# A banded attention with a feed-forward block on one core: operands of TensorE moved by a few words inside SBUF

## The chip, the cores and the metric

The kernel runs on one core of one Trainium2 chip. The metric is the device time of one execution in microseconds (us). "Word" below means 4 bytes, "place" means the start address of an operand in a partition of SBUF modulo 256 bytes, given in words (0 to 63).

## The reference

```python
scores = scale * (q @ k.T)                     # B=4, H=8, S=768, D=64
keep = (pos_k < n_sink) | (0 <= pos_q - pos_k < window)   # 4 sinks, window 128
a = softmax(where(keep, scores, -1e9)); x = a @ v          # x: 3072 tokens x 512
h = x @ w_in                                   # 512 -> 2048
out = (h - tanh(h)) @ w_out                    # 2048 -> 512
```

All operands are float32.

## The kernel before, in words

The 3072 tokens are cut into 12 chunks of 256. A chunk's attention makes its activations x, transposed (4 blocks of 128 features by 256 tokens). They are split into a rounded high part and a low part, `xh` and `xl`, and both lie in one half of the tile `xall` (chunk 2 alone has tiles of its own). A chunk then goes through 8 steps, one for each group of 256 hidden features. 96 steps `n` follow one another; `order` lists them: first chunks 0 to 2, taken in turn, then chunks 3 to 11, each with its 8 groups.

The first product of a step (`mm1`, L807) is 24 matmuls of 128x128 by 256 columns: a block of `w_in` is loaded as weights, and a block of `xh` or `xl` is streamed past it. Chunks 0 to 2 read `w_in` from tiles that stay in SBUF (`w0_g`). The later chunks get it by DMA into a ring of 7 slots, four in the tile `ring`, three in `spare`. ScalarE and VectorE then make the gate h - tanh(h) and split it again (`gate`): into `ghbuf` (high) and `glbuf` (low).

The second product has two forms. In steps of chunks 0 to 4, and in the last step (`mm2`, L877, 12 matmuls of 512 columns), halves of `ghbuf` and `glbuf` are the weights, and `w_out` is streamed. Steps with even `n` use the first half of `glbuf`, steps with odd `n` the second (`halves`). In the other steps (`mm7`, L911, 21 matmuls of 256 columns in a Strassen scheme) seven blocks of `ghbuf` and `glbuf` are the weights; blocks of `w_out` or of the tiles `edge` are streamed.

All instructions are recorded in a list with the engine, an estimated duration, a due time and the resources that they read and write. `Work.order` plays this list once and fixes the order of each engine; the waits between engines are then set by which bytes of a tile an instruction reads or writes. While one matmul streams, TensorE already loads the weights of the next one.

Places before, from the layout that the program is built with. `xall` begins at place 0. Chunks 0 and 1 lie 16 words into their half of it, so at place 16, and the chunks from 3 on at 0. The weights `w0_g` are at 0, but the tile that holds `w0_1` and later `ring` is at 16, as are `spare`, `ghbuf` and `glbuf`. `w_out` and the `edge` tiles are at 0. The key operands `ks` of the scores (L524) start at 0, 4, 32 or 36, their queries `q` at 16.

Of the kernel before, what the change touches and what calls it, by code (L numbers as in the profile page):

```python
# [9 lines left out]
F32 = mybir.dt.float32  # L10
F32R = mybir.dt.float32r
# [7 lines left out]
P = 128  # L19
# [20 lines left out]
@with_exitstack  # L40
def kernel(
    ctx: ExitStack,
    tc: tile.TileContext,
    qd: bass.AP,
    kp: bass.AP,
    vp: bass.AP,
    vs: bass.AP,
    nsw: bass.AP,
    w_in: bass.AP,
    w_out: bass.AP,  # L50
    xd: bass.AP,
    out: bass.AP,
):
    nc = tc.nc

    cpool = ctx.enter_context(tc.tile_pool(name="cpool", bufs=1))
    ident = cpool.tile([P, P], F32, tag="ident", name="ident")
    nswi = cpool.tile([P, 32], I32, tag="nswi", name="nswi")[:, :4]

    pts = cpool.tile([P, NPAIR, 2, 4, P], F32, tag="pt", name="pt")  # L60
    early = []
    for m in range(2):
        first = pts[:, m].rearrange("p h a b -> p (h a b)")
        early.append((first[:, :KW], first[:, KW : KW + 2 * CH].rearrange("p (h s) -> p h s", h=2)))
    et = mybir.EngineType
    with tc.manual_schedule(engines={et.PE, et.SP, et.DVE, et.Activation, et.Pool}):

        scr = pts[:, 2, 0]
        nc.sync.dma_start(nswi, nsw.partition_broadcast(P))
        for m in range(2):  # L70
            k, q = early[m]
            nc.sync.dma_start(k, kp[0, m, :, :KW])
            _load_pair(nc, q, qd[0, 2 * m : 2 * m + 2, :, :CH], True)
            if m == 0:
                make_identity(nc, ident)
                nc.gpsimd.iota(scr[:, 0, :].bitcast(I32), pattern=[[-1, P]], base=0, channel_multiplier=1)
                nc.gpsimd.iota(scr[:, 1, :].bitcast(I32), pattern=[[1, P]], base=0, channel_multiplier=0)
        masks = _masks(nc, cpool, nswi, scr)
        _, (nlo, nhi, wlo, whi) = nc.values_load_multi_w_load_instructions(
            nsw[0:1, 0:4], skip_runtime_bounds_check_because="every value takes one of the two branches"  # L80
        )
        bad = nhi | whi | ((nlo + 3) >> 3) | ((wlo - 1) >> 7)


        WARM = 3
        with tc.tile_pool(name="warm", bufs=1, space=PSUM) as wp:
            warm = wp.tile([P, P], F32, tag="warm", name="warm")
            for _ in range(WARM):
                nc.tensor.matmul(warm, lhsT=ident, rhs=ident, start=True, stop=True)

    with tc.If(bad == 0) as cmp:
        _banded(tc, qd, kp, vp, vs, masks, w_in, w_out, ident, pts, early, out)
    with cmp.Else():
        _general(tc, qd, kp, vp, nswi, w_in, w_out, ident, xd, out)

# [8 lines left out]
        nc.sync.dma_start(q[r, h, :], src[h, r])  # L104


def _masks(nc, pool, nswi, scr):

    mask = pool.tile([P, 3, TS], F32, tag="mask", name="mask")
    above = pool.tile([P, P], F32, tag="above", name="above")
    below = pool.tile([P, P], F32, tag="below", name="below")
    after = pool.tile([P, P], F32, tag="after", name="after")
    lim = pool.tile([P, 2], F32, tag="lim", name="lim")
    diff, col, tmp = (scr[:, i, :] for i in range(3))
    nc.gpsimd.memset(mask[:, 0, :NSK], NEG)
    nc.vector.tensor_copy(diff, diff.bitcast(I32))
    nc.vector.tensor_copy(col, col.bitcast(I32))  # L120
    nc.vector.tensor_scalar(above, diff, 0.0, None, op0=ALU.is_lt)
    nc.vector.tensor_scalar(below, diff, 0.0, None, op0=ALU.is_le)
    nc.vector.tensor_scalar(after, diff, 0.0, None, op0=ALU.is_gt)
    nc.vector.scalar_tensor_tensor(diff, above, float(P), diff, op0=ALU.mult, op1=ALU.add)
    nc.vector.tensor_scalar(tmp, above, NEG, None, op0=ALU.mult)
    nc.vector.tensor_copy(lim[:, 0:1], nswi[:, 0:1])
    nc.vector.tensor_copy(lim[:, 1:2], nswi[:, 2:3])
    n_sink, window = lim[:, 0:1], lim[:, 1:2]
    nc.vector.tensor_scalar(mask[:, 2, NSK:], diff, window, NEG, op0=ALU.is_ge, op1=ALU.mult)
    nc.vector.tensor_scalar(col, col, n_sink, NEG, op0=ALU.is_ge, op1=ALU.mult)  # L130
    nc.vector.tensor_tensor(mask[:, 0, NSK:], mask[:, 2, NSK:], tmp, op=ALU.min)
    nc.vector.tensor_tensor(mask[:, 0, NSK:], mask[:, 0, NSK:], col, op=ALU.max)

    near, edge, sink = diff[:, :NSK], tmp[:, :NSK], col[:, :NSK]
    nc.vector.tensor_scalar(near, near, window, None, op0=ALU.is_lt)
    nc.vector.tensor_tensor(edge, edge, near, op=ALU.mult)
    nc.vector.tensor_tensor(mask[:, 1, :NSK], edge, sink, op=ALU.min)

    def rest():
        nc.scalar.copy(mask[:, 1, NSK:], mask[:, 2, NSK:])  # L140
        nc.scalar.copy(mask[:, 2, :NSK], sink)

    return mask, above, below, after, rest
# [86 lines left out]
        return sorted(start, key=lambda n: (start[n], n)), start  # L230


def _banded(tc, qd, kp, vp, vs, masks, w_in, w_out, ident, pts, early, out):
    nc = tc.nc
    et = mybir.EngineType
    with ExitStack() as ctx:
# [6 lines left out]
        bpool, wmpool, qpool, kpool, hpool, xpool = (  # L243
            pool(n, 1) for n in ("bpool", "wmpool", "qpool", "kpool", "hpool", "xpool")
        )
        pp, sm = pool("pp", 2), pool("sm", 4)
        xall = xpool.tile([P, 4 * NPAIR * CH + 16], F32R, tag="xall", name="xall")
        ps, ps_h = pool("ps", 1, space=PSUM), pool("ps_h", 2, space=PSUM)
        dpool = pool("dpool", 1, space=bass.MemoryType.DRAM)

        banks = {n: ps.tile([P, 512], F32, tag=n, name=n) for n in ("s0", "s1", "o0", "o1", "t", "x")}
# [4 lines left out]
        flat = wide.rearrange("p a b c -> p (a b c)")  # L256
        gbuf = gpool.tile([P, 8, P], F32, tag="gbuf", name="gbuf")
        ghbuf = gpool.tile([P, 2, 7, P], F32R, tag="ghbuf", name="ghbuf")
        glbuf = gpool.tile([P, 8, P], F32R, tag="glbuf", name="glbuf")
        wscr = dpool.tile([NG, P, 2 * WG], F32, tag="wscr", name="wscr")  # L260
        bscr = dpool.tile([NG, P, 5, DM // 2], F32, tag="bscr", name="bscr")
        kscr = dpool.tile([2, P, 2, DM // 2], F32, tag="kscr", name="kscr")
# [150 lines left out]

        sides = cpool.tile([P, 4], F32, tag="sides", name="sides")
        sidei = cpool.tile([P, 16], I32, tag="sidei", name="sidei")[:, :4]
        half, odd = sides[:, 0:2], sides[:, 2:4]
        vsink = cpool.tile([P, 2, P], F32R, tag="vsink", name="vsink")
        vraw = cpool.tile([P, P], F32, tag="vraw", name="vraw")  # L420
# [86 lines left out]
        def scores(u, t):  # L507
# [134 lines left out]
        def attend(cc, p0, pairs):  # L642
# [35 lines left out]
            def x_high(i):  # L678
                if p0 == 0 and i == 0:
# [1 line left out]
                        xh[cc] = bpool.tile([P, NPAIR, CH], F32R, tag="hb", name=f"xh{cc}")  # L681
                        xl[cc] = hpool.tile([P, NPAIR, CH], F32R, tag="ha", name=f"xl{cc}")
                    else:
                        at = 2 * NPAIR * CH * (1 - home(cc)) + 16 * (cc < 3)
                        both = xall[:, at : at + 2 * NPAIR * CH].rearrange("p (k n c) -> p k n c", k=2, n=NPAIR)
                        xh[cc], xl[cc] = both[:, 0], both[:, 1]
                r = slice(p0 + 2 * i, p0 + 2 * i + 2)
# [126 lines left out]

        def halves(n):
            r = n % 2
            return ghbuf[:, r].rearrange("p b t -> p (b t)")[:, : 2 * CH], glbuf.rearrange("p b t -> p (b t)")[:, r * 2 * CH : (r + 1) * 2 * CH]

        def gate(n):
            g0 = gbuf.rearrange("p b t -> p (b t)")[:, : 2 * CH]  # L820
# [542 lines left out]
```

## Time and profile before

| | |
|---|---|
| time, median of 3 runs | 678.68 us (678.13, 678.68, 681.78) |
| profiled execution: span from first to last instruction | 676.2 us |
| what the median has beside that span | 2.5 us |
| TensorE busy with matmuls | 655.5 us (97%) |
| VectorE, ScalarE, GpSimd busy | 531.8, 412.6, 204.0 us |

The profile states no time for the profiled execution but its span; the 2.5 us are taken as what lies around it. Matmuls are pipelined: a row of a matmul gives a duration of some 280 ns for 256 columns, while the next begins some 115 ns after it. The distance from start to start (the "beat") is therefore read from the timeline, as the time between the starts of two rows divided by the matmuls between them. The duration of a single matmul follows the beat and is used where only durations are grouped.

### The profile page before, as it was taken

Reading aid. Unit: us, or ns where it says so; the run is one execution under the profiler, and the core shown is the slowest. Engines: PE = TensorE matmul, PEld = TensorE weight load, DVE = VectorE, ACT = ScalarE, POOL = GpSimd, SP = SyncE. Lnnn points to the kernel's source line nnn. Section 1 sums busy time; section 2 is a strip of 40 time slices with the busy share of each in tenths; the row PEclk is TensorE's granted clock in tenths of the full one; section 3 lists DMA queues with packets and bytes.
Section 4 is the critical chain, followed back from the end, with each engine's and each line's share of the span. In section 5 each row is a group of like instructions: output and inputs, shape, how many; then the busy total and the mean of one; then the engine's idle time right before and its main releaser. Section 6 shows DMA issues by size and latency. Waiting matters only on the chain.

```text
span 676.2 us, 14570 instructions
## 1 busy us (share of the span) xinstructions
PE 655.5 (97%) x5099; PEld 603.3 (89%) x5099; DVE 531.8 (79%) x1365; ACT 412.6 (61%) x1056; POOL 204.0 (30%) x363
## 2 busy tenths in 40 slices
PE   6899999999999999999999999999999999999995
PEld 4677899998988899889999999999999999999995
DVE  6889998964898975567798898888988878855654
ACT  4986443435998876556776667567667567632331
POOL 5454000001995443344523323332223322300100
PEclk9999999999999999999999999999999999999998
DMA  5878797786998677799977767867777766657861
GB/s 177 266 262 269 266 295 263 270 287 175 191 203 274 203 217 223 227 280 266 300 217 240 224 199 207 260 196 203 227 231 216 242 199 199 198 165 207 270 198 37
DMA packets 79341, 152.96 MB, mean 226 GB/s; under 512 B 9564, under 2 KB 25564, under 8 KB 79260
## 3 DMA queue, kind: packets, MB, share of 16 engines
q1 hardware_dynamic: 65884, 121.65, 57.4%
q0 software_dynamic: 13376, 30.30, 16.4%
q8 instruction: 42, 0.69, 0.4%
q14 instruction: 39, 0.32, 0.1%
HBM read 131.47 MB, written 20.45 MB: 225 GB/s over the span
## 4 chain that ended last, share of the span: by engine, by line
PE 73%; ACT 7%; DVE 5%; DMA 5%; POOL 4%; issue 4%; POOLq 0%; SPq 0%; DVEq 0%; ACTq 0%
PE h L807 30%; PE s L911 10%; PE o L911 7%; PE o L877 6%; PE x L672 3%; PE s L877 3%; DMA w<-bscr 2%; PE t L609 2%; PE t L672 2%; PE t L877 2%; PE t L524 2%; PE x L877 2%; ACT p L575 2%; PE x L524 1%; ACT p L549 1%
## 5 line engine op out<-in xcount | busy, mean ns | idle before, releaser
L807 PE MATMUL h<-xall,ring 128*128 128x256 f32 x990 | 130.9, 279 | 0.0
L807 PEld LDWEIGHTS h<-xall,ring 128*128 128x128 f32 x990 | 121.2, 188 | 0.9 <-PE t L672 0.2
L826 ACT ACTIVATE gbuf<-h 128x512 f32<-128x512 f32 x96 | 57.1, 595 | 84.6 <-PE h L807 55.2
L356 POOL DMA_DIRECT2D qraw<-qd x36 | 29.3, 813 | 222.4 <-DVE q L496 198.0
L807 PE MATMUL h<-xall,spare 128*128 128x256 f32 x738 | 96.2, 277 | 0.0
L807 PEld LDWEIGHTS h<-xall,spare 128*128 128x128 f32 x738 | 90.0, 188 | 0.5
L549 ACT ACTIVATE p<-p,st 128x132 f32<-128x132 f32 x168 | 66.9, 400 | 26.8 <-DVE st L541 25.5
L845 ACT CAST ghbuf<-gbuf 128x896 fp32r<-128x896 f32 x55 | 51.9, 943 | 49.3 <-DVE gbuf L842 48.8
L848 DVE TENSOR_TENSOR glbuf<-gbuf,ghbuf 128x896 fp32r<-128x896 f32 x55 | 60.3, 1096 | 19.7 <-ACT ghbuf L845 16.0
L575 ACT ACTIVATE p<-p,st 128x132 f32<-128x132 f32 x168 | 54.2, 394 | 3.9 <-DVE st L570 3.5
L829 DVE TENSOR_TENSOR gbuf<-h,gbuf 128x512 f32<-128x512 f32 x55 | 37.8, 687 | 19.1 <-ACT gbuf L826 18.7
L877 PE MATMUL o<-w,ghbuf 128*128 128x512 f32 x192 | 50.8, 399 | 0.3
L629 POOL TENSOR_TENSOR pt<-pt,after 128x512 f32<-128x512 f32 x32 | 44.4, 1386 | 22.0 <-ACT pt L626 21.3
L807 PE MATMUL h<-xall,w 128*128 128x256 f32 x384 | 50.5, 282 | 0.0
L807 PEld LDWEIGHTS h<-xall,w 128*128 128x128 f32 x384 | 48.5, 188 | 1.6
L829 DVE TENSOR_TENSOR h<-h,gbuf 128x512 f32<-128x512 f32 x41 | 28.5, 694 | 19.1 <-ACT gbuf L826 19.0
L488 DVE TENSOR_TENSOR ks<-kraw,ks 64x392 fp32r<-64x392 f32 x72 | 40.4, 562 | 3.4 <-ACT ks L483 1.1
L877 PEld LDWEIGHTS o<-w,ghbuf 128*128 128x128 f32 x192 | 33.8, 188 | 6.8 <-ACT ghbuf L832 0.9
L623 DVE TENSOR_TENSOR pt<-t,below 128x512 f32<-128x512 f32 (+1 forms) x48 | 28.8, 600 | 12.6 <-PE t L609 7.4
L483 ACT CAST ks<-kraw 64x392 fp32r<-64x392 f32 x72 | 37.1, 515 | 2.2 <-DMA kraw<-kp 1.4
L911 PE MATMUL s<-edge,ghbuf 128*128 128x256 f32 x220 | 35.5, 280 | 0.1
L835 DVE TENSOR_TENSOR glbuf<-h,ghbuf 128x512 fp32r<-128x512 f32 x41 | 28.1, 685 | 9.1 <-ACT ghbuf L832 9.1
(174 smaller groups left out, 1560.8 us busy)
## 6 DMA issues: line engine op xcount, KB each, us to landing
ring<-wscr SPq DMA_DIRECT2D x165, 256.0 KB, 4.3
spare<-wscr SPq DMA_DIRECT2D x123, 256.0 KB, 4.6
qraw<-qd POOLq DMA_DIRECT2D x36, 256.0 KB, 5.0
wraw<-w_in SPq DMA_DIRECT2D x16, 512.0 KB, 6.0
wraw<-w_out SPq DMA_DIRECT2D x16, 512.0 KB, 5.7
wscr<-w SPq DMA_DIRECT2D x16, 512.0 KB, 6.0
kraw<-kp POOLq DMA_DIRECT2D x36, 196.0 KB, 4.6
v<-vp POOLq DMA_DIRECT2D x18, 256.0 KB, 3.4
```

The lines of the kernel that those rows point to most:

```text
L483: nc.scalar.copy(ks[u][r, h, :], kt[u][r, :])
L488: (nc.gpsimd if KP else nc.vector).tensor_tensor(k[o, h, :], t[r, :], k[r, h, :].bitcast(F32), op=ALU.subtract)
L549: nc.scalar.activation(e, e, AF.Exp, bias=st[u][:, j : j + 1], scale=-1.0, accum_out=st[u][:, 4 + j : 5 + j],)
L575: nc.scalar.activation(pr[u][:, j, :], pr[u][:, j, :], AF.Copy, scale=s[:, 8 + j : 9 + j])
L629: nc.gpsimd.tensor_tensor(w[:, :, 0, :], w[:, :, 0, :], after.unsqueeze(1).to_broadcast([P, 4, P]), op=ALU.mult)
L807: nc.tensor.matmul(hps[n][:, f, :], lhsT=w, rhs=x, start=r == 0, stop=r == 11)
L826: nc.scalar.activation(g0, h(), AF.Tanh)
L829: nc.vector.tensor_tensor(g0 if strassen(n) else h(), h(), g0, op=ALU.subtract)
L845: nc.scalar.copy(ghbuf[:, n % 2], gbuf[:, 1:, :])
L848: nc.vector.tensor_tensor(glbuf[:, :7, :], gbuf[:, 1:, :], ghbuf[:, n % 2].bitcast(F32), op=ALU.subtract)
L877: nc.tensor.matmul(sums_of(n, cc, t), lhsT=a[:, f, t * P : (t + 1) * P], rhs=wt[1, g][:, (0, 1, 0)[i], f, :], start=first and not low and ...
L911: nc.tensor.matmul(acc, lhsT=a[:, b, :], rhs=factor(g, m, part % 2), start=g == 0 and part == 0 and m in (4, 1, 2, 7), stop=closes(n) and ...
```

## The change

The change moves tiles and slices, and leaves every computation as it is.

- Activations: the chunk's slice in `xall` starts at `xoff(cc)` words: chunks 0 and 1 at 48 (16 before), the chunks 3 to 11 at 1, 36, 2, 46, 16, 43, 20, 42 and 24 (0 before). `xall` is 32 words longer. Slices of neighbouring chunks do not overlap.
- Halves of the gate (steps with `mm2` alone): both halves start `shift(n)` words later, with 32, 30, 28, 26 and 4 in turn, so at places 48, 46, 44, 42 and 20 (16 before). `glbuf` gets 32 more words and another pool. The blocks that `mm7` reads stay at 16.
- Room for that: four small tiles (`lim`, `sides`, `sidei`, one of the four `st`) become slices of the tile of `nswi`, and the other three `st` become one tile.

```diff
-    nswi = cpool.tile([P, 32], I32, tag="nswi", name="nswi")[:, :4]
+    small = cpool.tile([P, 32], I32, tag="nswi", name="nswi")
+    nswi = small[:, :4]
...
-    lim = pool.tile([P, 2], F32, tag="lim", name="lim")
+    nswi, lim = small[:, :4], small[:, 4:6].bitcast(F32)
...
-        xall = xpool.tile([P, 4 * NPAIR * CH + 16], F32R, tag="xall", name="xall")
+        SHIFT, XOFF = 32, 48
+        xall = xpool.tile([P, 4 * NPAIR * CH + XOFF], F32R, tag="xall", name="xall")
...
+        stats = sm.tile([P, 3, 12], F32, tag="st", name="st")
+        glflat = cpool.tile([P, SHIFT + 8 * P], F32R, tag="glbuf", name="glbuf")
+        glbuf = glflat[:, : 8 * P].rearrange("p (b t) -> p b t", b=8)
...
-        glbuf = gpool.tile([P, 8, P], F32R, tag="glbuf", name="glbuf")
...
+        def xoff(cc):
+            return (48, 48, 0, 1, 36, 2, 46, 16, 43, 20, 42, 24)[cc]
+
+        def shift(n):
+            return (32, 30, 28, 26, 4)[n % 5]
...
-                    st[u] = sm.tile([P, 12], F32, tag="st", name=f"st{u}")
+                    st[u] = stats[:, u % 4] if u % 4 < 3 else small[:, 20:32].bitcast(F32)
...
-                        at = 2 * NPAIR * CH * (1 - home(cc)) + 16 * (cc < 3)
+                        at = 2 * NPAIR * CH * (1 - home(cc)) + xoff(cc)
...
             r = n % 2
-            return ghbuf[:, r].rearrange("p b t -> p (b t)")[:, : 2 * CH], glbuf.rearrange("p b t -> p (b t)")[:, r * 2 * CH : (r + 1) * 2 * CH]
+            a, b = shift(n), shift(n) + r * 2 * CH
+            return ghbuf[:, r].rearrange("p b t -> p (b t)")[:, a : a + 2 * CH], glflat[:, b : b + 2 * CH]
```

The order of instructions on every engine is the same; what is new is 18 waits. The two halves of `glbuf` were apart before. Now, where the shift changes from one step to the next, the half that VectorE writes in a step can share 2 to 28 words with the half that TensorE reads for the step before. The rows that follow are VectorE's around the low part of the gate in step 7 (`glbuf<-h`), of the kernel before:

```order
L829 TENSOR_TENSOR h_1204<-h_1204,gbuf 128x512 [waits Activation_49]
L158 SCALAR_TENSOR_TENSOR pt<-wraw_4_975,pt 128x1024 [waits DVE_49]
L835 TENSOR_TENSOR glbuf<-h_1204,ghbuf 128x512 [waits Activation_49]
L160 SCALAR_TENSOR_TENSOR pt<-wraw_4_975,pt 128x1024 [waits DVE_49]
L156 TENSOR_SCALAR pt<-wraw_4_1030 128x1024 [waits DMAHW3_49,DMAHW7_49,DMAHW2_49,DMAHW0_49]
```

The same place of the changed kernel:

```order
L840 TENSOR_TENSOR h_1190<-h_1190,gbuf 128x512 [waits Activation_49]
L159 SCALAR_TENSOR_TENSOR pt<-wraw_4_961,pt 128x1024 [waits DVE_49]
L846 TENSOR_TENSOR glbuf<-h_1190,ghbuf 128x512 [waits PE_49,Activation_49]
L161 SCALAR_TENSOR_TENSOR pt<-wraw_4_961,pt 128x1024 [waits DVE_49]
L157 TENSOR_SCALAR pt<-wraw_4_1016 128x1024 [waits DMAHW3_49,DMAHW7_49,DMAHW2_49,DMAHW0_49]
```

Nothing moved, but the low part now waits for TensorE as well; 16 of the 41 low parts of `mm2` steps do. The decoding of weights (`pt<-wraw`) is queued behind it. In two other steps (17 and 33) the low part stands ahead of the matmuls that read the other half, and there the last of these matmuls waits for VectorE. On TensorE, at the end of the second product of step 16, the changed kernel has:

```order
L888 MATMUL x<-w_7_1597,ghbuf 128x512 x4
L888 MATMUL t<-w_7_1597,glbuf 128x512 [waits DVE_49]
L888 MATMUL t<-w_7_1597,glbuf 128x512
L888 MATMUL x<-w_7_1597,glbuf 128x512
L888 MATMUL x<-w_7_1597,glbuf 128x512 [waits DVE_49]
```

The last two rows were one row `x2` without a wait.

## Rows read from the trace of the kernel before

**Rows 1.** The page: span and TensorE's busy time, its granted clock.

```profile
span 676.2 us, 14570 instructions
...
PEclk9999999999999999999999999999999999999998
```

**Rows 2.** Windows: us of window, busy us of each engine (instructions), clock.

```profile
77.50:202.40 124.90, 123.79 (x822) 110.75 (x822) 101.37 (x188) 69.65 (x162) 34.14 (x49) 1.00 0.82 244
202.40:318.00 115.60, 115.05 (x812) 102.35 (x811) 83.66 (x241) 80.76 (x221) 50.05 (x84) 1.00 0.81 239
318.00:664.00 346.00, 344.79 (x3036) 334.56 (x3036) 275.88 (x701) 204.90 (x484) 87.74 (x151) 1.00 0.72 218
```

**Rows 3.** Groups of TensorE: count, busy us, mean ns of one, idle before.

```profile
L807 PE MATMUL h<-xall,ring 128*128 128x256 f32 x990 | 130.9, 279 | 0.0
L807 PE MATMUL h<-xall,spare 128*128 128x256 f32 x738 | 96.2, 277 | 0.0
```

**Rows 4.** TensorE's timeline, chunk 10: start, us, what, count.

```profile
609.60 0.84 PE L807 MATMUL h<-xall,spare 128*128 128x256 f32 x6
610.28 2.20 PE L807 MATMUL h<-xall,ring 128*128 128x256 f32 x18
612.32 0.62 PE L911 MATMUL s<-edge,ghbuf 128*128 128x256 f32 x4
...
614.70 0.84 PE L807 MATMUL h<-xall,ring 128*128 128x256 f32 x6
```

**Rows 5.** TensorE's timeline, chunk 5, step 42.

```profile
334.47 0.87 PE L807 MATMUL h<-xall,ring 128*128 128x256 f32 x6
335.17 1.58 PE L807 MATMUL h<-xall,spare 128*128 128x256 f32 x12
336.59 0.63 PE L911 MATMUL s<-edge,ghbuf 128*128 128x256 f32 x4
337.06 0.40 PE L911 MATMUL o<-edge,ghbuf 128*128 128x256 f32 x2
```

**Rows 6.** TensorE's timeline, chunk 1, step 13.

```profile
126.92 2.99 PE L807 MATMUL h<-xall,w 128*128 128x256 f32 x24
129.75 1.10 PE L877 MATMUL t<-w,ghbuf 128*128 128x512 f32 x4
```

**Rows 7.** Line 807 by operands: count, min/median/max ns; whole late stretch, then step 42.

```profile
L807 PE MATMUL h<-xall,ring x990: 276/276/388, 205.0 to 663.5; 128*128 128x256 f32 x198
L807 PE MATMUL h<-xall,spare x738: 276/276/374, 209.1 to 662.8; 128*128 128x256 f32 x185
...
L807 PE MATMUL h<-xall,spare x12: 281/281/281, 335.2 to 336.5; 128*128 128x256 f32 x12
```

**Rows 8.** Line 807 by operands, 77.5 to 212, then step 4 (75.9 to 81.3).

```profile
L807 PE MATMUL h<-xall,w x306: 276/279/365, 77.8 to 192.7; 128*128 128x256 f32 x153
L807 PE MATMUL h<-xh,w x112: 274/279/284, 81.8 to 148.9; 128*128 128x256 f32 x112
L807 PE MATMUL h<-xl,w x56: 279/283/290, 81.9 to 148.8; 128*128 128x256 f32 x56
...
L807 PE MATMUL h<-xall,w x24: 276/282/283, 76.1 to 81.2; 128*128 128x256 f32 x24
```

**Rows 9.** Line 524 by operands, 202 to 664.

```profile
L524 PE MATMUL t<-ks,q x96: 277/283/396, 279.6 to 580.7; 128*128 128x260 f32 x96
L524 PE MATMUL x<-ks,q x96: 278/283/385, 279.9 to 580.9; 128*128 128x260 f32 x96
```

**Rows 10.** Line 877 by operands, 60 to 318.

```profile
L877 PE MATMUL o<-w,ghbuf x177: 388/394/502, 59.8 to 315.9; 128*128 128x512 f32 x177
L877 PE MATMUL s<-w,ghbuf x64: 390/394/401, 64.6 to 160.5; 128*128 128x512 f32 x64
```

**Rows 11.** Timelines of VectorE and TensorE, step 7.

```profile
98.54 0.68 DVE L835 TENSOR_TENSOR glbuf<-h,ghbuf 128x512 fp32r<-128x512 f32 x1
...
98.25 0.63 PE L877 MATMUL x<-w,glbuf 128*128 128x512 f32 x2
...
103.43 1.09 PE L877 MATMUL s<-w,glbuf 128*128 128x512 f32 x4
```

**Rows 12.** Timelines of VectorE and TensorE, steps 17 and 16.

```profile
155.09 0.69 DVE L835 TENSOR_TENSOR glbuf<-h,ghbuf 128x512 fp32r<-128x512 f32 x1 [0.65 <-ACT ghbuf L832]
...
155.60 0.63 PE L877 MATMUL x<-w,glbuf 128*128 128x512 f32 x2
```

More of the change, by code (lines that the diff above doesn't have):

```diff
@@ L77 @@
                 nc.gpsimd.iota(scr[:, 1, :].bitcast(I32), pattern=[[1, P]], base=0, channel_multiplier=0)
-        masks = _masks(nc, cpool, nswi, scr)
+        masks = _masks(nc, cpool, small, scr)
         _, (nlo, nhi, wlo, whi) = nc.values_load_multi_w_load_instructions(
@@ L91 @@
     with tc.If(bad == 0) as cmp:
-        _banded(tc, qd, kp, vp, vs, masks, w_in, w_out, ident, pts, early, out)
+        _banded(tc, qd, kp, vp, vs, small, masks, w_in, w_out, ident, pts, early, out)
     with cmp.Else():
@@ L104, in _load_pair, with _masks @@
         nc.sync.dma_start(q[r, h, :], src[h, r])
-def _masks(nc, pool, nswi, scr):
+def _masks(nc, pool, small, scr):
     mask = pool.tile([P, 3, TS], F32, tag="mask", name="mask")
@@ L230, in order, with _banded @@
         return sorted(start, key=lambda n: (start[n], n)), start
-def _banded(tc, qd, kp, vp, vs, masks, w_in, w_out, ident, pts, early, out):
+def _banded(tc, qd, kp, vp, vs, small, masks, w_in, w_out, ident, pts, early, out):
     nc = tc.nc
@@ L245, in _banded @@
         )
-        pp, sm = pool("pp", 2), pool("sm", 4)
-        xall = xpool.tile([P, 4 * NPAIR * CH + 16], F32R, tag="xall", name="xall")
+        pp, sm = pool("pp", 2), pool("sm", 1)
+        SHIFT, XOFF = 32, 48
+        xall = xpool.tile([P, 4 * NPAIR * CH + XOFF], F32R, tag="xall", name="xall")
         ps, ps_h = pool("ps", 1, space=PSUM), pool("ps_h", 2, space=PSUM)
+        stats = sm.tile([P, 3, 12], F32, tag="st", name="st")
+        glflat = cpool.tile([P, SHIFT + 8 * P], F32R, tag="glbuf", name="glbuf")
+        glbuf = glflat[:, : 8 * P].rearrange("p (b t) -> p b t", b=8)
         dpool = pool("dpool", 1, space=bass.MemoryType.DRAM)
@@ L412, in _banded @@
             qt[u], kt[u] = q, k
-        sides = cpool.tile([P, 4], F32, tag="sides", name="sides")
-        sidei = cpool.tile([P, 16], I32, tag="sidei", name="sidei")[:, :4]
+        sides = small[:, 8:12].bitcast(F32)
+        sidei = small[:, 16:20]
         half, odd = sides[:, 0:2], sides[:, 2:4]
```

## The prediction, made before the changed kernel ran

> **What bounds the kernel now.** I read the page first: TensorE is busy for nearly the whole span, at the full granted clock (2.4 GHz) up to the last slice [rows 1]. The windows say where: from 77.5 to 202.4 us it is busy 123.79 of 124.90 us, from 202.4 to 318 us 115.05 of 115.60, from 318 to 664 us 344.79 of 346.00 [rows 2]. VectorE, the next, has 19% of the first stretch to spare and more of the others. So the time is the number of matmuls times the beat from one start to the next, and every ns on a beat is paid in full. The change has no other lever: it moves no instruction and only changes places, so the question is whether the beat depends on places.
>
> It does, or on something that goes with them. In chunk 10 two steps start 5.10 us apart (609.60 and 614.70) with 24 + 21 matmuls between, a beat of 113.3 ns [rows 4]. In step 13, which has the same matmul with other places (activations at 16 words, weights at 0), 24 matmuls take from 126.92 to 129.75, a beat of 117.9 ns [rows 6]. No engine is waited for in either. The durations follow: 276 ns on the fast beat, 279 to 282 on the slow one [rows 7, 8]. But places are not all. In step 42 the places are those of chunk 10, and 18 matmuls take from 334.47 to 336.59, 117.8 ns each, 281 ns long [rows 5, 7]. There is thus a fast and a slow beat, and at the places of the late chunks both can hold, the fast one nearly always: the median of all late matmuls is its 276 ns [rows 7].
>
> Of the places that the trace shows, only activations at 0 with weights at 16, 16 words behind the weights, are fast. At 16 with weights at 0 the median is 279; at 0 with weights at 0 (`xl` of chunk 2) 283; at 16 with weights at 16 (step 4) 282 [rows 8]. The score matmuls, with keys at 0, 4, 32 and 36 and queries at 16, have 283 [rows 9]; their 4 more columns are worth 4/256 of 113 ns, 2 ns, so these are slow as well, though they come in runs too short to settle.
>
> **The change part by part.** The sum is made on the span of 676.2 us; the median lies 2.5 us above it, and that is added at the end.
>
> *First products of the nine late chunks.* 990 + 738 = 1728 matmuls, 192 a chunk [rows 3]. What they take now: the means are 277 ns at `spare` and 279 at `ring`, where single ones behind a wait last up to 388 [rows 3, 7]. I take the 277, 1 ns above the fast duration, so a mean beat of 114.3. On the slow beat a chunk loses 117.8 - 114.3 = 3.5 ns x 192 = 0.67 us. None of the new places is shown by the trace except one: chunk 7, at 16 with weights at 16, is the case of step 4, which is slow. Measured by the distance to the weights, chunks 3 and 5 (at 1 and 2) move from -16 to -15 and -14, next to the fast place; chunks 7, 9 and 11 (16, 20, 24) go to 0, +4 and +8; chunk 4 (36) to +20; chunks 10, 8 and 6 (42, 43, 46) to +26, +27 and +30. At 0 and +16 the rows are slow, so I count 7, 9, 11 and 4 as slow. Of +26 to +30 nothing is known, and I count them with the nearest row, +16. Seven slow chunks: 7 x 0.67 = +4.7 us. Bounds: all nine slow, +6.0; all on the fast beat without a slip, 1728 x 1 ns = -1.7.
>
> *Second products behind them.* The 21 matmuls of a step in chunks 5 to 11 keep their places and could run fast, but step 42 shows that a slow beat is handed on: after its first product, 4 matmuls of L911 take from 336.59 to 337.06, 117.5 ns [rows 5]. Six of the seven slow chunks have this form: 6 x 8 steps x 21, about 1000 matmuls. If a quarter stays slow: 250 x 3.5 ns = +0.9 us. Bounds 0 and 3.5 us.
>
> *Chunks 0 and 1.* They move from 16 to 48 with weights at 0, so from a distance of +16 to +48, which is -16 modulo 64: the distance of the late chunks. 306 matmuls of this kind lie in the stretch where TensorE bounds [rows 2, 8], 24 of them (step 4) with weights at 16. The other 282 gain 117.9 - 113.3 = 4.6 ns, -1.3 us. Bounds: nothing; or, if they become as `xl` of chunk 2, 283 for 279 ns, +4 ns, +1.1 us. I take -1.3, as the distance is the only reading that I use above.
>
> *The halves of the gate.* 41 steps x 12 = 492 matmuls of 512 columns, whose weights move from 16 to 20 and 42 to 48. Their median is 394 ns in every stretch and whatever their neighbours are, between 388 and 401 apart from waits [rows 10]. A matmul twice as long covers the load of the next weights for longer, so I take 0. Bounds: all at the shortest, 492 x 6 = -3.0 us; all at the longest, 492 x 7 = +3.4 us.
>
> *The 18 new waits.* In step 7 the low part starts on VectorE at 98.54, and the matmuls that read the other half end at 98.25 + 0.63 = 98.88: a wait of 0.34 us. Behind it stands the decoding of weights, and its own reader starts only at 103.43, 4.2 us after the low part ends [rows 11]. VectorE has 23 us to spare in that stretch [rows 2], so this is hidden: 0. Without that cover, 16 waits of 0.34 us would be 5.4 us. Where TensorE waits, in step 16, the low part ends at 155.09 + 0.69 = 155.78, and the second of the two matmuls from 155.60 on would start at about 155.83 [rows 12]: 0, at most some 0.1 us. The merged small tiles change no instruction, 0.
>
> Sum: 4.7 + 0.9 - 1.3 = +4.3; 676.2 + 4.3 + 2.5 = 683.0 us.
>
> **A rule against this.** The late chunks and step 13 run the same matmul at 113.3 and 117.9 ns with nothing else waited for [rows 4, 6]. The Trainium skill, TensorE: Matmul & The Clock Gate, section "Step-by-step: what each phase is for", says that TensorE has two independent read ports into SBUF and that loading the next weights takes no bandwidth from the running matmul. By that rule places would be worth nothing, and the sum would be 0: that is the first rival, and the trace bears it out only in so far as both beats occur at the same places.
>
> **The rivals.**
>
> *Places do not decide.* The beat is set by how loads and matmuls fall against one another after a wait, and the places only happen to differ between the stages. For it: step 42 [rows 5]. Against it: step 13 and its like stay slow throughout, and the late chunks return to 276 after each disturbance [rows 7, 8]. The time is then 678.7, give or take 1.5 us.
>
> *Only a start at a multiple of 256 bytes is fast.* For it: every row with activations at 16 is slow, whatever the weights [rows 8]. Against it: `xl` of chunk 2 starts at 0 and is slow, with weights at 0. Then all nine chunks lose, +6.0 us; a quarter of all second products follows, 1155 x 1/4 x 3.5 = +1.0; chunks 0 and 1 gain nothing. 676.2 + 7.0 + 2.5 = 685.7 us, and 688.7 if all second products follow.
>
> *The new places are the better ones* (the other side). Most late chunks hold the fast beat without a slip (-1.7), the second products slip less with them (1155 x 1 ns, -1.2), chunks 0 and 1 gain 1.3, and the halves come near their shortest duration (up to -3.0). That is 674.5 without the halves and 671.5 with them. It decides from the point where no more than one of the nine is slow and the halves give 1 us or more. Against it: nothing in the trace is below 276 ns for long, so there is little to win, and each place that is shown, other than today's, is slow.
>
> **How the numbers follow.** The forecast (four to seven chunks slow) has 0.38, 680.5 to 685.5; the rule of 256 bytes 0.20, 685 to 689; no effect of places 0.24, 677 to 680.5; better places 0.18, 671 to 676. A change of under 0.5%, 3.4 us, cannot be told from none, so faster is below 675.3 and slower above 682.1. Faster: most of the last case, 0.15. Slower: two thirds of the first and nearly all of the second, 0.25 + 0.19 = 0.44. The rest, 0.41, is no change. The range that leaves out no more than 2 in 10 goes from 674 to 687.5.
>
> **What would show it.** Grouped by chunk, the first products should have a median of 276 ns in chunks 3 and 5 and of 281 in 4, 7, 9 and 11; chunks 6, 8 and 10 decide between 680.5 and the full sum. Step 13 should take 2.72 us for its 24 matmuls, not 2.83. The 512-column rows should stay at 394, and idle time of TensorE before `glbuf` should not grow. The prediction is wrong if the durations of the late chunks do not move, if they fall below 276, or if the 512-column matmuls change by more than 2 ns.

## The result, and the profile after

The changed kernel takes 685.59 us (median of 7 runs, 683.02 to 687.03), the kernel before in the same comparison 679.59 us. The ratio is 1.0083, 95% interval 1.0056 to 1.0110: slower by 0.8%. The profiled span grew from 676.2 [rows 1] to 683.8 us. In every run on record the time lies 1.7 to 1.9 us above the span, so the profiled execution of the kernel before took about 678.1 us, the lowest of its seven runs (678.13). Some 0.6 of the 2.5 us that the prediction adds are therefore that execution's distance from the median. It lies 1.5 us below the median of the seven, which is why the spans differ by 7.6 us and the medians by 6.0.

The windows of the changed kernel, cut at the same steps as before (columns as in rows 2):

```profile
76.80:201.30 124.50, 122.91 (x822) 109.99 (x820) 101.83 (x188) 69.52 (x161) 33.87 (x49) 1.00 0.81 245
201.30:318.00 116.70, 116.28 (x806) 103.83 (x807) 83.30 (x239) 81.24 (x222) 50.34 (x84) 1.00 0.81 236
318.00:671.50 353.50, 352.95 (x3041) 343.10 (x3040) 276.97 (x703) 204.56 (x484) 87.21 (x151) 1.00 0.70 214
```

Against [rows 2] the three stretches changed by -0.4, +1.1 and +7.5 us. The granted clock is 1.00 in all (2.4 GHz) as before and TensorE's busy time grew with the stretch, so the loss is in the late steps and in the beat. By operands, the page of after (columns as in rows 3):

```profile
L817 PE MATMUL h<-xall,ring 128*128 128x256 f32 x990 | 135.8, 284 | 0.0
...
L817 PE MATMUL h<-xall,spare 128*128 128x256 f32 x738 | 100.1, 283 | 0.0
...
L817 PE MATMUL h<-xall,w 128*128 128x256 f32 x384 | 49.8, 281 | 0.0
```

L817 is L807 of before. The late first products went from 279 and 277 ns [rows 3] to 284 and 283. Chunk by chunk (count, min/median/max ns, first and last start; chunks 3 to 11 in turn, `ring` alone):

```profile
L817 PE MATMUL h<-xall,ring x120: 278/283/362, 204.2 to 258.7; 128*128 128x256 f32 x120
...
L817 PE MATMUL h<-xall,ring x102: 277/281/362, 264.8 to 314.9; 128*128 128x256 f32 x102
...
L817 PE MATMUL h<-xall,ring x114: 279/283/365, 318.3 to 368.2; 128*128 128x256 f32 x114
...
L817 PE MATMUL h<-xall,ring x110: 278/285/366, 374.2 to 422.7; 128*128 128x256 f32 x110
...
L817 PE MATMUL h<-xall,ring x110: 274/283/364, 422.4 to 474.1; 128*128 128x256 f32 x110
...
L817 PE MATMUL h<-xall,ring x114: 276/282/384, 479.7 to 528.1; 128*128 128x256 f32 x114
...
L817 PE MATMUL h<-xall,ring x104: 275/280/365, 531.1 to 580.5; 128*128 128x256 f32 x104
...
L817 PE MATMUL h<-xall,ring x120: 278/284/364, 580.4 to 629.3; 128*128 128x256 f32 x120
...
L817 PE MATMUL h<-xall,ring x102: 277/280/357, 633.9 to 671.0; 128*128 128x256 f32 x102
```

No chunk kept the 276 of [rows 7]: none of the nine places holds the fast beat for a chunk. The beat itself, in chunk 10 (TensorE's timeline of after, answering to rows 4):

```profile
605.52 1.60 PE L817 MATMUL h<-xall,spare 128*128 128x256 f32 x12
606.96 1.60 PE L817 MATMUL h<-xall,ring 128*128 128x256 f32 x12
608.40 0.62 PE L922 MATMUL s<-edge,ghbuf 128*128 128x256 f32 x4
...
610.78 1.60 PE L817 MATMUL h<-xall,ring 128*128 128x256 f32 x12
```

The 24 first products take 2.88 us, 120.0 ns each, and the 21 second products behind them 2.38 us, 113.3 ns. In this chunk the loss sits on the matmuls whose operand was moved, and on no other.

The other direction, step 13, which answers to rows 6:

```profile
125.97 2.89 PE L817 MATMUL h<-xall,w 128*128 128x256 f32 x24
128.70 1.08 PE L888 MATMUL t<-w,ghbuf 128*128 128x512 f32 x4
```

2.73 us for 24 matmuls where it was 2.83, a beat of 113.8 ns. Step 19, at the same places, has 117.8 ns for 18 matmuls (160.42 to 162.54):

```profile
160.42 2.29 PE L817 MATMUL h<-xall,w 128*128 128x256 f32 x18
162.54 0.64 PE L534 MATMUL s<-ks,q 128*128 128x260 f32 x4
```

So at 48 past weights at 0 both beats occur. Of the 14 steps of chunks 0 and 1 past weights at 0, nine have 113.3 to 114.9 ns and five 117.4 to 117.9 (the first two distances of each left out); before, all 14 were at 117.5 to 117.9. VectorE's new waits (line waited for: us in total, times, longest):

```profile
DVE glbuf L846 <- PE o L888: 3.9, 3, 1.5
...
DVE glbuf L846 <- PE x L888: 1.0, 3, 0.4
```

Its wait for `ghbuf` at the same line fell from 9.1 to 7.1 us. TensorE waits for `glbuf` as long as before, 0.8 us once (before, then after):

```profile
PE t L877 <- DVE glbuf L835: 0.8, 1, 0.8
...
PE t L888 <- DVE glbuf L846: 0.8, 1, 0.8
```

From here on a beat is a mean over the distances from one start to the next, with the distances that hold a wait left out; I worked them out from the timelines. The beats explain the loss:

| matmuls | count | before | after | us |
|---|---|---|---|---|
| first products, chunks 3 to 11 | 1728 | 114.19 | 119.34 | +8.9 |
| second products behind them (L922) | 1155 | 114.11 | 115.25 | +1.3 |
| first products, chunks 0 and 1 | 384 | 117.88 | 115.79 | -0.8 |
| 512 columns, halves of the gate | 492 | 233.10 | 231.64 | -0.7 |

The sum is +8.7 us. The distances with a wait in them, which stand beside these, became about 1 us shorter in all, which leaves about the 7.6 us of the span. Two profiles of one kernel differ by about 1 us in the opening alone (before: the first product starts at 42.6 and at 41.5 us), so I read effects under 2 us from beats, not from spans.

### The profile page after: what moved, and what is told of

It reads as the page before. It is cut to its first block, busy times and chain, and to the rows that moved or that the text cites. A ratio compares the mean times of both kernels' runs of the same rounds, so it can differ in the third digit from the quotient of the medians.

```text
span 683.8 us, 14585 instructions
## 1 busy us (share of the span) xinstructions
PE 664.5 (97%) x5099; PEld 613.7 (90%) x5099; DVE 532.3 (78%) x1365; ACT 412.8 (60%) x1056; POOL 204.0 (30%) x363
## 4 chain that ended last, share of the span: by engine, by line
PE 80%; DVE 6%; ACT 4%; DMA 3%; POOL 3%; issue 2%; SPq 0%; POOLq 0%; DVEq 0%; ACTq 0%
PE h L817 35%; PE s L922 11%; PE o L922 8%; PE o L888 7%; PE x L682 3%; PE s L888 3%; PE t L619 2%; PE t L534 2%; PE t L682 2%; PE t L888 2%; PE x L534 2%; PE x L888 2%; DMA kraw<-kp 2%; DMA w<-bscr 1%; DVE pt L633 1%
## 5 line engine op out<-in xcount | busy, mean ns | idle before, releaser
L817 PE MATMUL h<-xall,ring 128*128 128x256 f32 x990 | 135.8, 284 | 0.0
L817 PEld LDWEIGHTS h<-xall,ring 128*128 128x128 f32 x990 | 125.3, 189 | 0.8 <-PE t L682 0.2
L817 PE MATMUL h<-xall,spare 128*128 128x256 f32 x738 | 100.1, 283 | 0.0
L817 PEld LDWEIGHTS h<-xall,spare 128*128 128x128 f32 x738 | 93.3, 190 | 0.5
L559 ACT ACTIVATE p<-p,st 128x132 f32<-128x132 f32 x132 | 52.6, 401 | 21.7 <-DVE st L551 20.6
L817 PE MATMUL h<-xall,w 128*128 128x256 f32 x384 | 49.8, 281 | 0.0
L817 PEld LDWEIGHTS h<-xall,w 128*128 128x128 f32 x384 | 47.8, 188 | 1.5
L585 ACT ACTIVATE p<-p,st 128x132 f32<-128x132 f32 x132 | 42.6, 394 | 3.2 <-DVE st L580 2.8
L922 PE MATMUL s<-edge,ghbuf 128*128 128x256 f32 x220 | 35.9, 282 | 0.0
```

Source lines behind the costliest of these rows:

```text
L559: nc.scalar.activation(e, e, AF.Exp, bias=st[u][:, j : j + 1], scale=-1.0, accum_out=st[u][:, 4 + j : 5 + j],)
L585: nc.scalar.activation(pr[u][:, j, :], pr[u][:, j, :], AF.Copy, scale=s[:, 8 + j : 9 + j])
L817: nc.tensor.matmul(hps[n][:, f, :], lhsT=w, rhs=x, start=r == 0, stop=r == 11)
L922: nc.tensor.matmul(acc, lhsT=a[:, b, :], rhs=factor(g, m, part % 2), start=g == 0 and part == 0 and m in (4, 1, 2, 7), stop=closes(n) and ...
```

## The experiments

All but e5_before_again and g1_high48 are the changed kernel with other numbers in `xoff` (first line of each diff: places of chunks 0 to 11) and `shift` (second line: 0 keeps the halves at 16, 32 puts them at 48, 28 at 44); e4_ring32 has a line more. What most gave stands in one table (beats in ns); "all" is the median time, with the 95% interval of the ratio to the kernel before where the two were timed side by side.

| kernel | all, us | 95% of the ratio | late first | second | chunks 0, 1 | 512 col. | chunk 10, 11 |
|---|---|---|---|---|---|---|---|
| before | 679.59 | | 114.19 | 114.11 | 117.88 | 233.10 | 113.7, 113.4 |
| after | 685.59 | 1.0056 to 1.0110 | 119.34 | 115.25 | 115.79 | 231.64 | 119.9, 116.8 |
| e1_late_only | 685.32 | 1.0057 to 1.0183 | 119.34 | 115.20 | 117.87 | 233.22 | 120.0, 116.8 |
| e2_rest_only | 680.28 | 0.9997 to 1.0050 | 115.37 | 115.46 | 115.79 | 231.65 | 117.0, 117.8 |
| e7_rest_again | 680.61 | one run | 115.25 | 115.43 | 116.01 | 231.61 | 117.0, 117.8 |
| v1_adopt | 679.35 | 0.9984 to 1.0029 | 115.02 | 114.89 | 116.75 | 230.63 | 117.0, 115.0 |
| f1_early_only | 680.00 | 0.9991 to 1.0040 | 114.76 | 114.97 | 115.99 | 233.00 | 117.0, 115.0 |
| f2_halves_only | 679.42 | 0.9977 to 1.0017 | 115.31 | 115.40 | 117.85 | 230.63 | 116.8, 117.8 |
| f3_old_places | 680.95 | 1.0003 to 1.0044 | 114.78 | 114.89 | 117.85 | 233.09 | 116.7, 115.1 |
| g1_high48 | 679.43 | 0.9965 to 1.0016 | 114.64 | 114.65 | 117.97 | 231.30 | 113.7, 116.1 |
| e5_before_again | 676.95 | one run | 114.17 | 114.05 | 117.87 | 233.18 | 113.5, 114.0 |

**The late places alone (e1_late_only).**

```diff
-            return (48, 48, 0, 1, 36, 2, 46, 16, 43, 20, 42, 24)[cc]
+            return (16, 16, 0, 1, 36, 2, 46, 16, 43, 20, 42, 24)[cc]
...
-            return (32, 30, 28, 26, 4)[n % 5]
+            return (0, 0, 0, 0, 0)[n % 5]
```

> One part alone: the nine late chunks lie at 1, 36, 2, 46, 16, 43, 20, 42 and 24 words as in the changed kernel; chunks 0 and 1 are back at 16, the halves of the gate at 16. Theory (the late first products are the whole loss, and the other two parts give something back): in the changed kernel the 1728 late first products have a mean beat of 119.3 ns against 114.2 before, +8.8 us, and the second products behind them +1.4 us; without what chunks 0 and 1 and the halves give back (1.4 us) the kernel is some 9 us slower than before, about 1.013, with the same beats by chunk as in the changed kernel. Rival (the loss comes from the new waits on the halves of glbuf, or from the halves' places): then this kernel, which has neither, is within 0.3% of before.

Ratio 1.0120. Every chunk has the beat that it has in after, within 0.3 ns, and the early and the 512-column matmuls are those of before. The moved late activations are thus the loss, whatever else the change does.

**Everything but the late places (e2_rest_only), and the same again (e7_rest_again).**

```diff
-            return (48, 48, 0, 1, 36, 2, 46, 16, 43, 20, 42, 24)[cc]
+            return (48, 48, 0, 0, 0, 0, 0, 0, 0, 0, 0, 0)[cc]
```

> The other part alone: the late chunks are back at 0; chunks 0 and 1 at 48, the halves of the gate at 48, 46, 44, 42 and 20 in turn, with the 18 waits. Theory: late first products at 114 ns again, chunks 0 and 1 at 115 to 116 ns (118 before), 512-column matmuls at 232 ns (233 before): 1.4 us faster than before, a ratio of about 0.998. Rival (the waits cost): over 1.003 times before, with idle time of VectorE or TensorE before glbuf.

The two gains are there (115.79 and 231.65 ns), -1.5 us by beats, but the time is not below that of before: chunks 10 and 11, at place 0 as before, run slowly. e2_rest_only, chunk 10:

```profile
604.35 1.58 PE L817 MATMUL h<-xall,ring 128*128 128x256 f32 x12
605.76 1.58 PE L817 MATMUL h<-xall,spare 128*128 128x256 f32 x12
...
609.65 0.87 PE L817 MATMUL h<-xall,spare 128*128 128x256 f32 x6
```

5.30 us for the 45 matmuls that took 5.10 in [rows 4]: 117.8 ns, and here the second products too.

> The kernel with the other parts alone (late chunks at 0), profiled a second time. Theory D1 (chance of the execution): chunks 10 and 11 need not be at 117.8 ns again. Theory D2 (fixed by the program): they are, within 0.5 ns.

It came again in both chunks to 0.1 ns; and the kernel before, profiled again, stayed fast in both:

> The kernel before, unchanged, profiled a second time. Theory D1 (the beat of a late chunk is chance of the single execution: DMA landings and the like): the mean beats by chunk differ from the first profile, some chunk from 8 to 11 by 2 ns or more. Theory D2 (it is fixed by the program): they are the same to 0.5 ns, 113.7 and 113.4 ns in chunks 10 and 11.

So this long slow stretch is no accident of one execution. That does not hold for every stretch. In chunk 10, step 1, six first products and the four second products behind them begin 118 ns apart in the kernel before (588.25 to 589.43) and 113 ns apart in e5_before_again (587.16 to 588.29):

```profile
588.25 0.87 PE L807 MATMUL h<-xall,ring 128*128 128x256 f32 x6
588.96 0.63 PE L911 MATMUL s<-w,ghbuf 128*128 128x256 f32 x4
589.43 0.63 PE L911 MATMUL o<-w,ghbuf 128*128 128x256 f32 x4
...
587.16 0.84 PE L807 MATMUL h<-xall,ring 128*128 128x256 f32 x6
587.84 0.62 PE L911 MATMUL s<-w,ghbuf 128*128 128x256 f32 x4
588.29 0.62 PE L911 MATMUL o<-w,ghbuf 128*128 128x256 f32 x4
```

The same program thus mostly, but not always, gets the same beat in the same stretch.

**Other late places (e3_fours, e6_lines).** Diffs to after:

```diff
-            return (48, 48, 0, 1, 36, 2, 46, 16, 43, 20, 42, 24)[cc]
+            return (48, 48, 0, 4, 32, 8, 40, 12, 44, 28, 48, 32)[cc]
...
-            return (32, 30, 28, 26, 4)[n % 5]
+            return (32, 32, 32, 32, 32)[n % 5]
```

> All late chunks at multiples of 4 words (16 bytes), weights at 16 as before: chunks 3 to 11 at 4, 32, 8, 40, 12, 44, 28, 48 and 32; halves of the gate all at 48. Theory A (a start off a multiple of 16 bytes costs on its own: the chunks at 1, 2, 42, 43 and 46 had beats of 119.4 to 121.4 ns, those at 16, 20, 24 and 36 116.8 to 119.2): here every chunk is at 119 or below, those at 40 and 44 too, though 42 and 43 had 119.9 and 119.4. Theory B (the distance to the weights decides, and only near -16 it is fast): 4 and 8 (distances -12 and -8) are the fastest, 114 to 116, and 40, 44 and 48 stay at 119 to 121 like their neighbours. Theory C (only a start at a multiple of 256 bytes can hold the fast beat): all nine at 117 or above.

Time 684.68 us. Beats of chunks 3 to 11: 118.9, 116.3, 118.2, 119.6, 117.2, 116.9, 118.3, 118.9, 118.0. Places 4 and 8, a whole number of 16 bytes behind the fast one, are slow: theory B falls, and theory A, with 119 at most, fails at 40 (119.6). Theory C just misses (116.3 and 116.9). The 116.3 of chunk 4, at place 32, is a mean of both beats: four of its eleven longer runs are at 113.6 to 113.9 ns, the others at 117.5 to 118.0; chunk 11, at 32 as well, has the slow beat alone. One of the four takes 113.9 ns (311.68 to 313.73, 18 matmuls):

```profile
311.68 2.21 PE L817 MATMUL h<-xall,spare 128*128 128x256 f32 x18
313.73 0.60 PE L619 MATMUL t<-ident,p 128*128 128x128 f32 x4
```

```diff
-            return (48, 48, 0, 1, 36, 2, 46, 16, 43, 20, 42, 24)[cc]
+            return (48, 48, 0, 16, 36, 17, 37, 18, 38, 19, 39, 20)[cc]
...
-            return (32, 30, 28, 26, 4)[n % 5]
+            return (28, 28, 28, 28, 28)[n % 5]
```

> Late chunks at 16, 17, 18, 19 and 20 (chunks 3, 5, 7, 9, 11) and at 36, 37, 38 and 39 (4, 6, 8, 10), weights at 16; halves of the gate at 44. Theory A (a start off a multiple of 4 words costs on its own): 16 and 20 at 117 to 119.5 ns, 17, 18 and 19 at 120.5 to 122.5; 36 at 118.6, 37 to 39 at 120 or more. Rival (single places are better or worse without such a rule): no such step, 17 to 19 lie between 16 and 20.

Time 684.24 us. Beats: 16: 119.2, 17: 122.2, 18: 118.4, 19: 117.4, 20: 118.4; 36: 118.9, 37: 122.1, 38: 119.9, 39: 118.8. That a start off a multiple of four words costs more is wrong as a rule: 18 and 19 are no worse than 16 and 20. One word past a multiple of four stands out (17, 37, and 1 with 121.3 in after), but 46, two words past, had 121.4 there.

**The weights moved instead (e4_ring32).** `ring` goes to place 32, `spare` stays at 16, so that each chunk shows one place against two.

```diff
-            return (48, 48, 0, 1, 36, 2, 46, 16, 43, 20, 42, 24)[cc]
+            return (48, 48, 0, 0, 16, 0, 17, 16, 32, 16, 48, 1)[cc]
...
-            return (32, 30, 28, 26, 4)[n % 5]
+            return (32, 32, 32, 32, 32)[n % 5]
...
-                return rpool.tile([P, FAR + 2 * WG], dtype, tag="w0_1", name=name)[:, FAR:]
+                return rpool.tile([P, FAR + 2 * WG], dtype, tag="w0_1", name=name)[:, 32 : 32 + 2 * WG]
```

> The ring's weights are moved from 16 to 32 words; those in spare stay at 16, so that each chunk meets both. Chunks 3 and 5 at 0; 4, 7 and 9 at 16; 6 at 17; 8 at 32; 10 at 48; 11 at 1. Theory B (distance -16 is fast wherever it lies): chunks 4, 7 and 9 are fast (113 to 115 ns) in the ring and slow (118 or more) in spare, and chunks 3 and 5 slow in the ring and fast in spare. Theory C (the start of the activations decides): chunks 3 and 5 are fast in both, all others slow in both. Theory A adds that 6 and 11 (17 and 1 words) are slower than 7 and 9 by 2 ns or more, in ring and spare alike.

Time 683.2 us. Chunk 3 (activations at 0) and chunk 4 (at 16), by operands:

```profile
L817 PE MATMUL h<-xall,ring x120: 274/281/367, 203.6 to 257.4; 128*128 128x256 f32 x120
L817 PE MATMUL h<-xall,spare x72: 276/276/287, 207.8 to 251.4; 128*128 128x256 f32 x72
...
L817 PE MATMUL h<-xall,ring x102: 276/281/367, 263.4 to 313.2; 128*128 128x256 f32 x102
L817 PE MATMUL h<-xall,spare x90: 276/283/364, 260.8 to 312.0; 128*128 128x256 f32 x90
```

The same activations at 0 are fast past weights at 16 (beat 114.9) and slow past weights at 32 (118.4): where the weights lie counts too, so a start at a multiple of 256 bytes is not enough. 16 past 32 has the distance of 0 past 16, and a mean of 117.0 where 16 past 16 has 119.3. This mean too hides two beats: of ten runs of 11 or more matmuls, three are at 114.2 to 114.6 ns (their first distance left out) and seven at 117.8 to 118.2. One of the three takes 115 ns (465.42 to 466.80, 12 matmuls):

```profile
465.42 1.54 PE L817 MATMUL h<-xall,ring 128*128 128x256 f32 x12
466.80 0.41 PE L534 MATMUL t<-ks,q 128*128 128x260 f32 x2
```

The same count over all kernels gives: the fast beat occurs at the three pairs with the distance of -16 words modulo 64, which are 0 past 16 (575 of 735 runs under 115 ns), 48 past 0 (about half of the steps) and 16 past 32. Elsewhere, chunk 2 aside, only 32 past 16 (4 of 23 runs) and 20 past 16 (2 of 24) show it; 16 past 0, 16 past 16 and 0 past 32 never do. The distance of -16 thus lets the fast beat in without ensuring it, and one word off it (1 past 16) is among the slowest.

**The gains without waits (v1_adopt).** The diff of e2_rest_only, and `shift` 32 for all steps, whose halves then do not overlap.

> A version that keeps what gave something back: late chunks at 0 as before, chunks 0 and 1 at 48, both halves of the gate at 48 in every step, so that they lie apart again and none of the 18 waits is there. If first products at 0 always ran on the fast beat: chunks 0 and 1 at 115 to 117 ns instead of 118, 384 matmuls, -0.8 us; 492 matmuls of 512 columns at 230.6 instead of 233.1 ns, -1.2 us; together 0.3% faster than before, ratio 0.997. Theory D (two beats at the same places, and which one holds depends on what went before): the late chunks can stay on the slow beat for whole chunks, as chunks 10 and 11 did in the kernel with the other parts alone (117.8 ns); that takes up to 1.7 us for these two with their second products, and the result is anything from 0.995 to 1.003. Rival to D (the 18 waits or the halves' places set the late beat): with one place for all halves and no waits, chunks 10 and 11 are fast, 113 to 114 ns.

The ratio is 1.0007: no better than before. The 512-column matmuls reach 230.63, and chunk 10 is slow all the same, so the new waits are not needed for it.

**One gain at a time (f1_early_only, f2_halves_only).** Chunks 0 and 1 at 48 with `shift` 0; then chunks 0 and 1 at 16 with `shift` 32; the late chunks at 0 in both.

> Chunks 0 and 1 at 48, everything else at the places of the kernel before (late chunks at 0, halves of the gate at 16, no new waits). The early products should go from 117.9 to between 115.8 and 116.8 ns, as in the two kernels that had them at 48: 384 x 1.6 ns = -0.6 us. Theory 1 (the halves at 48 are what put late chunks on the slow beat): chunks 10 and 11 stay at 113.4 to 113.7 as before, and the time is 0.5 to 1 us below the kernel before. Theory 2 (any change of places ahead of the late chunks can flip some of them): at least one late chunk is at 116 or more, and the time is that of before within 0.5 us.

> The halves of the gate at 48, everything else at the places of the kernel before (late chunks at 0, chunks 0 and 1 at 16). The 512-column matmuls should go from 233.1 to 230.6 ns as in the two kernels with all halves at 48: 492 x 2.5 = -1.2 us. Theory 1 (the halves at 48 put late chunks on the slow beat): chunk 10 or 11 goes from 113.5 to about 117, +0.7 us or more each with the second products behind, and the time is that of before within 0.5 us. Theory 2 (any change of places can flip some): one of the late chunks is slow too, but it need not be 10 or 11. If no late chunk is slow, the kernel should be 1 us faster than before, about the least that the comparison can show.

Both gains come alone (115.99; 230.63), and chunk 10 is slow in either. Theory 1 fell with f1; that left what all these kernels share.

**The new arrangement with the old places (f3_old_places).**

```diff
-            return (48, 48, 0, 1, 36, 2, 46, 16, 43, 20, 42, 24)[cc]
+            return (16, 16, 0, 0, 0, 0, 0, 0, 0, 0, 0, 0)[cc]
...
-            return (32, 30, 28, 26, 4)[n % 5]
+            return (0, 0, 0, 0, 0)[n % 5]
```

> The arrangement of the changed kernel (merged small tiles, the wider buffers, the other halves of the gate in a buffer of their own) with every activation and every half at the place of the kernel before. No place modulo 256 bytes differs from before, only where whole tiles lie. Theory 2 (a change of places ahead of the late chunks flips some of them): chunks 10 and 11 stay at 113.4 to 113.7 and the time is that of before. Theory 3 (what the four kernels with slow late chunks share is the new arrangement, and it alone flips them): chunk 10 is at about 117 here too, late products at 114.7 or more, second products at 114.8 or more, early ones 117.9 and the halves 233 as before, so a span about 2 us longer than that of before, and a median 1 to 2.5 us above it.

As theory 3 said: no place differs from before, and chunk 10 is at 116.7. The time is 1.0024 of before, 2.0 us; the beats give 1.9 us, of which 1.1 lie in chunk 10 and 0.5 in chunk 11. Chunk 10 is slow in all six profiles of the new arrangement with late chunks at 0, and fast in all three of the old one (before, e5_before_again and the next run). TensorE's timeline in chunk 10 shows where it turns:

```profile
589.92 0.84 PE L817 MATMUL h<-xall,ring 128*128 128x256 f32 x6
590.60 0.62 PE L922 MATMUL s<-w,ghbuf 128*128 128x256 f32 x4
...
592.06 1.96 PE L682 MATMUL x<-pt,v 128*64 128x256 f32 x24
593.85 1.91 PE L682 MATMUL t<-pt,v 128*64 128x256 f32 x24
...
596.61 1.58 PE L817 MATMUL h<-xall,ring 128*128 128x256 f32 x12
598.03 0.87 PE L817 MATMUL h<-xall,spare 128*128 128x256 f32 x6
```

Before the 48 attention matmuls the beat is 113.3 (0.68 us for 6), behind them 118 (1.42 for 12), and it stays at 117.8 in every step to the end of the chunk.

**The old arrangement with one gain (g1_high48).** In the kernel before, one line:

```diff
-            return ghbuf[:, r].rearrange("p b t -> p (b t)")[:, : 2 * CH], glbuf.rearrange("p b t -> p (b t)")[:, r * 2 * CH : (r + 1) * 2 * CH]
+            return ghbuf[:, r].rearrange("p b t -> p (b t)")[:, 32 : 32 + 2 * CH], glbuf.rearrange("p b t -> p (b t)")[:, r * 2 * CH : (r + 1) * 2 * CH]
```

> The kernel before, with nothing else in it moved, and the gate's high halves (328 of the 492 matmuls of 512 columns) 32 words further, at 48 instead of 16. Every tile lies where it lay. If a place is worth in this arrangement what it was in the other, these matmuls go from 233.1 to about 231 ns, 328 x 2.2 = -0.7 us. Theory 3 (the new arrangement is what slows chunk 10): chunks 10 and 11 stay at 113.4 to 114, late products at 114.2, and the span is about 0.7 us below that of before. Theory 2 (any change of places ahead of the late chunks flips some): chunk 10, 11 or another late chunk is at 116 or more, and the gain is eaten. Either way the time is within 0.2 per cent of before.

The moved halves go from 233.1 to 230.4, chunk 10 stays at 113.7 as theory 3 wants, and now chunk 11 turns slow, as theory 2 wants. Its timeline:

```profile
634.96 1.52 PE L807 MATMUL h<-xall,spare 128*128 128x256 f32 x12
636.32 1.52 PE L807 MATMUL h<-xall,ring 128*128 128x256 f32 x12
638.39 0.94 PE L807 MATMUL h<-xall,ring 128*128 128x256 f32 x6 [0.55 <-DMA ring<-wscr]
...
641.65 0.87 PE L807 MATMUL h<-xall,ring 128*128 128x256 f32 x6
642.36 1.58 PE L807 MATMUL h<-xall,spare 128*128 128x256 f32 x12
643.77 0.63 PE L911 MATMUL s<-edge,ghbuf 128*128 128x256 f32 x4
```

113.3 ns until a wait of 0.55 us for a weight slot, and 117.8 from there to the end (641.65 to 643.77, 18 matmuls). This is one profile, and single stretches differ between two profiles of one kernel as well, so it is not shown that the edit turned chunk 11.

What the profiles have in common is that the beat changes at interruptions alone. I went through the nine profiles with late chunks at 0 for stretches of 18 or more first and second products of 256 columns with no other matmul and no distance over 135 ns in them. There are 403. In 402, past the first six matmuls and taken six by six, one beat holds to the end: the fast one in 330, the slow one in 72. The longest slow one has 630 matmuls (e2_rest_only, chunks 10 and 11). The one change inside a stretch (v1_adopt at 638.8 us) comes right behind a matmul that started 123 ns after the last. So after an interruption TensorE comes back on either beat, and keeps it until the next one. What picks the beat is not shown. In chunk 10 it goes with the arrangement of the tiles; in some shorter stretches it differs between two executions of one program. The ratio of g1_high48 is 0.999, interval 0.9965 to 1.0016: no version here is shown to beat the kernel before.

## Why the prediction was right or wrong

The time, 685.6 us, is slower, as forecast, and inside the stated range; it lies just above the forecast case (680.5 to 685.5) and in the span of the rule of 256 bytes (685 to 689). The mechanism, late first products on a slower beat, was the forecast's. The size was not: the beats give +8.7 us for +4.3. That the median came within 2.6 us of 683.0 is in part luck, as it grew by only 6.0 us. Step by step:

- *Bound and lever*: right. TensorE is busy throughout in both kernels and the clock is the same; the time went where the beats went.
- *Late first products*: the mechanism was right, the term was mis-sized, +8.9 us for +4.7. Two steps of it failed. "Measured by the distance to the weights" chunks 3 and 5 were counted as next to the fast place; they are among the slowest (283 ns, 121.3 and 120.4) and cost 6.8 and 6.0 ns x 192 = 2.5 us. And the slow beat was taken as one level, 117.8; at the other seven places it is 116.8 to 121.4, and they cost 6.4 us instead of 4.7. The bound "all nine slow, +6.0" rested on the same level and was too low as well. 117.8 is the slow beat at 0 past 16; other places can be worse. A chunk's beat can also be a mean of both: chunk 9, at 20, has 113.3 ns in most of one step (540.5 to 543.1) and 116.5 to 118.5 in the others.
- *Second products*: +1.3 for +0.9, right in size. That a slow beat is handed on is only part of it: in the step of chunk 10 above they run at 113.3 right behind a first product at 120.0, while in chunks 5 to 9 they are at 115.0 to 116.3.
- *Chunks 0 and 1*: -0.8 for -1.3. The distance of -16 did what it was taken for, but in nine of 14 steps only; step 13 does as forecast, step 19 does not. (24 matmuls a chunk past weights at 16 are at 119.) That both beats can hold at one pair was read in step 42, but not allowed for in this term.
- *Halves*: forecast 0, measured -0.7 by beats and inside the bounds. The median duration stayed at 394 in most groups, as forecast (392 in two), and here the duration misled: the gain shows from start to start.
- *18 waits*: right. 4.9 us on VectorE, nothing more on TensorE (0.8 us, as before).
- *The merged tiles and the moved buffer, "0"*: not safe. f3_old_places, which is that edit alone, has 1.0024 of the time of before (1.0003 to 1.0044), chiefly from chunks 10 and 11 turning slow. In after, where no late chunk lies at the fast place, its share can't be told apart.

The rivals. "Places do not decide" is refuted as to the sum: e1_late_only and f3_old_places have the same arrangement and instructions, and 119.34 against 114.78 ns, 1728 x 4.56 = 7.9 us. But what it described in part exists, a beat that is settled at an interruption and then kept, and it is what ate the gains in five kernels (e2, v1, f1, f2, g1); that loads falling against matmuls is the reason is not shown. "Only a start at a multiple of 256 bytes is fast" gave 685.7, the nearest time, and its main term held (nine of nine slow). That was luck: its +6.0 was +8.9, and its rule did not hold: chunks 0 and 1 gained at 48, 32 past 16 and 16 past 32 can run fast, and 0 past 32 is slow. "The new places are better" fell in all late chunks.

The Trainium skill's rule weighed there (TensorE: Matmul & The Clock Gate, "Step-by-step: what each phase is for") says that loading the next weights takes no SBUF read bandwidth from the running matmul. What the prediction drew from it, that places are worth nothing, does not hold here: in e4_ring32 the same activations have 276 or 281 ns by the place of the weights alone. Whether bandwidth is what they share is not shown.

What stays open: why the distance of -16 words lets the fast beat in, why 1, 17, 37 and 46 are the worst, what in an interruption picks the beat, and why the new arrangement slows chunk 10. That places count modulo 256 bytes was assumed; 48 past 0 agrees with it, and no run was made to test it.

## What to carry to other kernels

Where TensorE is busy without a gap and loads weights for each 256 columns, the places of both operands modulo 256 bytes are worth up to 8% of the beat, and a few measured pairs say more than any rule worked out from two or three. Read beats from start to start, by group; a median duration can hide 1%, and a mean beat can hide two beats. Before a gain of 0.1 to 0.2% is credited to an edit, look at whether an unrelated stretch has turned to the other beat, and time the rearrangement alone, at the old places.

## What was not expected of the hardware

- At the same places (0 past 16) two sharp beats exist, 113.3 and 117.8 ns for 128x128 weights and 256 columns, and each holds over whole steps, first and second products alike (chunk 10 of f3_old_places and e2_rest_only: 5.30 us a step; of before and g1_high48: 5.10 us).
- Which one holds is settled at an interruption, such as 48 attention matmuls or a wait of 0.55 us, and then kept (402 of 403 stretches). Long stretches came out alike in two executions of one program (before: chunk 10 at 113.7 and 113.5; e2: 117.0 and 117.0), some shorter ones did not (chunk 10, step 1: 118 and 113).
- The fast beat also occurs at 48 past 0 and 16 past 32, the same distance modulo 64 words, and in a few runs at 32 and 20 past 16.
- Activations at 1, 17, 37 and 46 past weights at 16 take 121 to 122 ns, at 16, 18, 19 and 20 117 to 119.
- Weights of 512-column matmuls at 48 instead of 16 give 230.4 to 230.6 ns for 233.1.
